# First-layer weights fetched for two column blocks at once, units in a matching order, key and value loads of two batches cut in two, and a new order for the opening

## The chip, the cores and the metric

The program runs on one core of one Trainium2 chip. The metric is the device time of one execution in microseconds (us); the time given for a kernel is the median of its runs. The engines are named as the profile names them: PE (TensorE, matrix products), DVE (VectorE), ACT (ScalarE), POOL (GpSimd) and SP (SyncE, which issues nearly all loads here).

## The reference, cut to what matters

```python
def sm_attn(qq, kk, vv):                       # softmax attention, scale = 1/8
    s = scale * np.matmul(qq, kk.transpose(0, 1, 3, 2))
    s = s - np.max(s, axis=-1, keepdims=True)
    a = np.exp(s)
    a = a / (np.sum(a, axis=-1, keepdims=True) + 1e-09)
    return np.matmul(a, vv)

p_packed = sm_attn(p, k, v)                    # q, k, v: 8 batches, 8 heads, 576, 64; p: 32 rows
out = sm_attn(q, p_packed, p_packed)
x = out.transpose(0, 2, 1, 3).reshape(4608, 512)
h = np.maximum(np.maximum(x @ w1, x @ w2), x @ w3)     # w1, w2, w3: 512 x 768
x = h @ w_out                                          # 768 x 512
...
h = x @ w_in                                           # 512 x 2048
g = np.maximum(h, 0.0) + np.log1p(np.exp(-np.abs(h)))
return g @ w_out                                       # 2048 x 512
```

All weights arrive as 64-bit floats, so each value is loaded as 8 bytes and narrowed on the chip.

## The kernel before

The attention and the first two layers run batch by batch (n = 0 to 7). For a batch, keys and queries are loaded (`load_raw`, L167), values too (`load_v`, L196). Head dimensions are brought onto the partitions: for the keys and queries of batch 0 and the keys of batch 1 (the set `BY_PE`) by PE products with the identity (L231), for all others by DVE (L253, L256). Then follow the scores of the packed rows (S, L286), the softmax (SX: DVE maximum L306, ACT exponential L312), its transposition (E, L330), the product with the values (V, L357), the scaling and transposition of the result (VS and PT, L373, L265) and the second scores (A, L286). The second softmax is a chain on DVE, ACT and POOL (AX: L397, L403, L405, L409, L423 to L434), and its result is split into a high and a low half (X, L127).

Because the packed result has only 32 rows a head, it is first multiplied into the weights of the first layer: `packed_weight_steps` (PW, L449, matmul L459) makes four 128-column blocks of "packed weights" at a time from the narrowed weights `wsb`, and splits them into `pwhi` and `pwlo`. `unit_steps` (U, L486) then makes one of 18 units, each one 128-column block f of one of the three matrices w, with 12 matmuls at L481. The maximum over the three matrices is kept in `m` (L508, L510), split into `hhi` and `hlo` (LS) and multiplied by `w_out` (L20 to L23: four column blocks of the second layer, 36 matmuls each).

The last two layers (from L959 on) follow for all batches together; the change does not touch them.

The weights come in 18 loads of 512 KB (`load_w`, L566), one for a pair (f, w): two 32-bit words a value, 256 words (1,024 bytes) in a row of the load, four rows a partition. Each is narrowed by an ACT step (L85), a POOL step (L95) and a DVE step (`combine`, L111). `w_out` comes in six loads of 512 KB (LO), with rows of 4,096 bytes. The raw loads of both share a pool of five buffers (`stp`), the raw keys and queries another of five (`rx`); so a load waits until the DVE step of the load five before it is over. All these loads stand in SP's queue.

For batch 0 and the part of batch 1 that overlaps it (called the opening here), the order of the work on every engine is written out by hand in the string `order` (L634): each word is the next step of a named piece of work (Lk10 loads keys of batch 1, heads 0; Tk10 turns them; LW21 loads a weight block, NT21 and N21 narrow it; U5 is a unit). Every engine keeps its own instructions in that order. `lead` adds idle PE products with the identity (L165) in front of a piece, `on_gpsimd` says which subtractions and products run on POOL. From batch 1 on, `small_work` (L700) sets the places of the pieces between the units.

The lines around the narrowing buffer and the units are these:

```python
wsb = wsbp.tile([P, 3 * F1, NH, P], F32, name="wsb")
c, k = divmod(3 * f + w, 4)
hi, lo = pw[n, c]
```

Of the kernel before, what the change touches and what calls it, by code (L numbers as in the profile page):

```python
# [19 lines left out]
def packed_attention_maxout_softplus(  # L20
# [22 lines left out]
    nc = tc.nc  # L43
# [107 lines left out]
    wsb = wsbp.tile([P, 3 * F1, NH, P], F32, name="wsb")  # L151
# [14 lines left out]

    def load_raw(n, g, which, queue=nc.sync):  # L167
# [5 lines left out]
        if (n, which) in BY_PE:  # L173
            queue.dma_start(
                out=t.rearrange("p t b d -> p (t b d)")[: 32 * TI, : NG * NI * D].rearrange(
                    "p (h c) -> p h c", h=NG
                ),
                in_=src[n, NG * g : NG * g + NG].rearrange("h (p r) d -> p h (r d)", r=NI),
            )
            raw[n, g, which] = t  # L180
            return
# [14 lines left out]
    def load_v(n, queue=nc.sync):  # L196
        t = vvp.tile([32 * TI, H, NI, D], F32, name="vt")
        queue.dma_start(
            out=t.rearrange("p h i d -> p h (i d)"),
            in_=v[n].rearrange("h (p r) d -> p h (r d)", r=NI),  # L200
        )
        vt[n] = t
# [246 lines left out]
    def packed_weight_steps(n, c):  # L449
# [5 lines left out]
        for g in range(NH):  # L455
            for G in range(NG):
# [3 lines left out]
                    ps[cols, G, : units * P].rearrange("p (w x) -> p w x", w=units),  # L460
                    ppT[n][rows, cols],
                    wsb[rows, 4 * c : 4 * c + units, g],
# [20 lines left out]
    def layer1_unit(n, f, w):  # L483
        every(unit_steps(n, f, w))

    def unit_steps(n, f, w):  # L486
        c, k = divmod(3 * f + w, 4)
# [78 lines left out]
    def load_w(f, w, queue=nc.sync):  # L566
        t = stp.tile([P, NH * P, 2], I32, tag="st", name="wraw")
        queue.dma_start(
            out=t.rearrange("p (g x) t -> p g (x t)", g=NH),
            in_=(w1, w2, w3)[w][:, f * 2 * P : f * 2 * P + 2 * P].rearrange(  # L570
                "(g p) x -> p g x", p=P
            ),
# [20 lines left out]
    def opening(name):  # L593
# [14 lines left out]
        if a == "U":  # L608
            return unit_steps(0, *divmod(int(num), 3))
# [22 lines left out]
    on_gpsimd.update("""AX00.sb AX00.mu AX01.mu SO5 SO0 AX10.sb AX11.sb AX10.mu X11""".split())  # L632
    lead.update({"Tk00": 11, "S0": 2, "V0": 1, "PT0": 2, "A0": 2, "Tk10": 12, "Tk13": 2, "PP1": 4, "S1": 3, "U0": 1})
    order = """  # L634
            Lk00 Lk02 Lp0 Lk01 Lk03 Lq00 Tk00 PP0 Tk00 Lq03 Tk02 PP0 Tk01 Tk02 Lq02 Lv0
# [549 lines left out]
```

## Time and profile before

| | us |
|---|---|
| median of 3 runs | 1254.85 |
| lowest and highest run | 1252.23, 1256.12 |
| the profiled execution, whole | 1258.63 |
| its span, first to last instruction | 1256.8 |
| PE busy in the span | 1240.9 (99%) |
| DVE busy in the span | 687.5 (55%) |
| PE waiting for values by DMA, its largest wait for one releaser in the first 260 us | 2.2 |

All durations below come from the profiled execution. A row of the timeline gives start, duration, engine, line, and behind it in brackets the time for which the engine stood idle and what released it. The clock column is the granted TensorE clock as a share of 2.4 GHz: 0.50 is 1.2 GHz. DMA is the mean busy share of the core's 16 DMA engines (it can pass 1 where transfers of one engine overlap).

### The profile page before, as it was taken

Reading aid. Unit: us, or ns where it says so; the run is one execution under the profiler, and the core shown is the slowest. Engines: PE = TensorE matmul, PEld = TensorE weight load, DVE = VectorE, ACT = ScalarE, POOL = GpSimd, SP = SyncE. Lnnn points to the kernel's source line nnn. Section 1 sums busy time; section 2 is a strip of 40 time slices with the busy share of each in tenths; the row PEclk is TensorE's granted clock in tenths of the full one; section 3 lists DMA queues with packets and bytes.
Section 4 is the critical chain, followed back from the end, with each engine's and each line's share of the span. In section 5 each row is a group of like instructions: output and inputs, shape, how many; then the busy total and the mean of one; then the engine's idle time right before and its main releaser. Section 6 shows DMA issues by size and latency. Waiting matters only on the chain.

```text
span 1256.8 us, 21080 instructions
## 1 busy us (share of the span) xinstructions
PE 1240.9 (99%) x8647; PEld 1065.2 (85%) x8647; DVE 687.5 (55%) x1070; ACT 463.4 (37%) x687; POOL 116.4 (9%) x112
## 2 busy tenths in 40 slices
PE   8989999999999999999999999999999999999998
PEld 6778989898999899888888888888888888888997
DVE  2965657575666649676663445634445354442443
ACT  4733443434343435454342222513224222232222
POOL 1412312122221301000000000000000000000000
PEclk9989999999999999999999999999999999999999
DMA  9967576879695722665522433415334053340641
GB/s 234 283 176 207 160 197 174 205 204 231 178 239 164 180 68 73 250 245 195 196 68 93 150 118 118 126 34 209 118 117 126 15 170 117 125 143 1 209 176 35
DMA packets 87008, 192.55 MB, mean 153 GB/s; under 512 B 12160, under 2 KB 56448, under 8 KB 81792
## 3 DMA queue, kind: packets, MB, share of 16 engines
q1 hardware_dynamic: 81920, 181.24, 48.2%
q10 hardware_dynamic: 4992, 9.96, 2.2%
q8 instruction: 68, 1.11, 0.4%
q14 instruction: 28, 0.23, 0.1%
HBM read 149.23 MB, written 41.94 MB: 152 GB/s over the span
## 4 chain that ended last, share of the span: by engine, by line
PE 94%; DMA 3%; DVE 1%; ACT 1%; issue 0%; ACTq 0%; POOL 0%; SPq 0%; DVEq 0%; POOLq 0%
PE ps L481 29%; PE ps L959 28%; PE acc L1033 10%; PE acc L1032 10%; PE acc L1031 10%; PE ps_w L459 3%; DMA qraw<-in_q_dram 2%; PE ps_s L286 1%; PE ps_v L357 1%; PE ps_e L330 1%; PE ps_k L231 1%; DMA wraw<-in_moe_w_dram 0%; DVE wsb L111 0%; DMA kraw<-in_k_dram 0%; DVE x2lo L127 0%
## 5 line engine op out<-in xcount | busy, mean ns | idle before, releaser
L959 PE MATMUL ps<-x2hi,wc 128*128 128x512 f32 (+1 forms) x1120 | 322.8, 369 | 0.0
L976 DVE TENSOR_TENSOR h<-h,ps 128x512 f32<-128x512 f32 (+1 forms) x280 | 173.9, 634 | 110.5 <-PE ps L959 105.0
L959 PEld LDWEIGHTS ps<-x2hi,wc 128*128 128x128 f32 x1120 | 203.6, 188 | 35.9
L1033 PE MATMUL acc<-w2hi,glo 128*128 128x512 f32 x576 | 224.8, 390 | 0.0
L1032 PE MATMUL acc<-w2lo,ghi 128*128 128x512 f32 x576 | 224.7, 390 | 0.0
L1031 PE MATMUL acc<-w2hi,ghi 128*128 128x512 f32 x576 | 224.1, 389 | 0.0
L959 PE MATMUL ps<-x2lo,wc 128*128 128x512 f32 (+1 forms) x560 | 206.5, 369 | 0.0
L127 DVE TENSOR_TENSOR glo<-h,ghi 128x512 fp32r<-128x512 f32 x80 | 54.9, 692 | 157.2 <-ACT ghi L125 157.2
L1032 PEld LDWEIGHTS acc<-w2lo,ghi 128*128 128x128 f32 x576 | 108.1, 188 | 23.2
L481 PE MATMUL ps<-a2hi,pwhi 128*128 128x288 f32 x576 | 127.6, 303 | 0.1
L1031 PEld LDWEIGHTS acc<-w2hi,ghi 128*128 128x128 f32 x576 | 108.2, 188 | 22.7
L1033 PEld LDWEIGHTS acc<-w2hi,glo 128*128 128x128 f32 x576 | 108.1, 188 | 22.6
L999 ACT ACTIVATE h<-h 128x1024 f32<-128x1024 f32 x40 | 42.4, 1060 | 230.2 <-DVE h L976 230.2
L481 PE MATMUL ps<-a2hi,pwlo 128*128 128x288 f32 x576 | 123.2, 296 | 0.4 <-DVE pwlo L127 0.4
L481 PE MATMUL ps<-a2lo,pwhi 128*128 128x288 f32 x576 | 123.2, 295 | 0.0
L959 PEld LDWEIGHTS ps<-x2lo,wc 128*128 128x128 f32 x560 | 105.5, 188 | 18.3
L481 PEld LDWEIGHTS ps<-a2hi,pwhi 128*128 128x128 f32 x576 | 91.6, 189 | 15.0 <-ACT m L508 5.3
L510 DVE TENSOR_TENSOR m<-ps,m 128x576 f32<-128x576 f32 x96 | 72.4, 754 | 48.9 <-PE ps L481 42.8
L481 PEld LDWEIGHTS ps<-a2hi,pwlo 128*128 128x128 f32 x576 | 92.6, 188 | 0.7 <-DVE pwlo L127 0.7
L481 PEld LDWEIGHTS ps<-a2lo,pwhi 128*128 128x128 f32 x576 | 92.5, 188 | 0.3 <-DVE a2lo L127 0.3
L127 DVE TENSOR_TENSOR pwlo<-ps_w,pwhi 128x1024 fp32r<-128x1024 f32 (+1 forms) x40 | 44.6, 1114 | 84.7 <-ACT pwhi L125 84.7
L127 DVE TENSOR_TENSOR glo<-gs,ghi 128x512 fp32r<-128x512 f32 x64 | 44.2, 691 | 79.1 <-ACT ghi L125 71.0
(105 smaller groups left out, 1495.6 us busy)
## 6 DMA issues: line engine op xcount, KB each, us to landing
wc<-wic SPq DMA_DIRECT2D x32, 1792.0 KB
qraw<-in_q_dram SPq DMA_DIRECT2D x112, 140.0 KB
wic<-wc SPq DMA_DIRECT2D x8, 1792.0 KB
kraw<-in_k_dram SPq DMA_DIRECT2D x96, 140.0 KB
vt<-in_v_dram SPq DMA_DIRECT2D x8, 1152.0 KB
wraw<-in_moe_w_dram SPq DMA_DIRECT2D x18, 512.0 KB
x2d<-xs ACTq DMA_DIRECT2D x32, 288.0 KB
xu<-x2d SPq DMA_DIRECT2D x72, 128.0 KB
```

What stands on the lines that cost most here:

```text
L127: engine.tensor_tensor(out=lo, in0=src, in1=hi.bitcast(F32), op=ALU.subtract)
L231: nc.tensor.matmul(ps[64 * G : 64 * G + 64, i // hi, c : c + rows], r[:, i, G], ident[:rows, :rows], start=True, stop=True,)
L286: nc.tensor.matmul(ps[G][cols, hh, :HS], w[rows, cols], x[rows, g, hh * HS : hh * HS + HS], start=True, stop=True,)
L459: nc.tensor.matmul(ps[cols, G, : units * P].rearrange("p (w x) -> p w x", w=units), ppT[n][rows, cols], wsb[rows, 4 * c : 4 * c + units, g ...
L481: nc.tensor.matmul(o, w, xx, start=first, stop=last)
L510: nc.vector.tensor_tensor(out=m, in0=ps[:, :, :HS], in1=ms[n, f], op=ALU.max)
L959: nc.tensor.matmul(out, l, r, start=(i == 0), stop=(i == len(terms) - 1))
L976: add(out=h[:, o], in0=h[:, a], in1=ps, op=ALU.add)
L999: nc.scalar.activation(out=out, in_=x, func=AF.Softplus)
L1031: nc.tensor.matmul(ps, ghi[:, cols], whi, start=first, stop=False)
L1032: nc.tensor.matmul(ps, ghi[:, cols], wlo, start=False, stop=False)
L1033: nc.tensor.matmul(ps, glo[:, cols], whi, start=False, stop=last)
```

## The change

- `wsb` holds two column blocks next to each other: 9 pairs d, and for each four row groups of 256 columns. `load_w(d, h)` fetches, for one matrix and a pair of column blocks, half of the 512 rows: still 18 loads of 512 KB, now with 512 words (2,048 bytes) in a row and two rows a partition.
- The units are numbered so that the two blocks of a pair alternate: unit u belongs to block `2 * (u // 6) + u % 2` and matrix `u // 2 % 3`. The splitting of a finished block (LS) moves accordingly, in all batches.
- `load_rows` cuts the loads of keys (heads pairs of batches 0 and 1) and values (batches 0 and 1) into a transfer of rows 4 p to 4 p + 3 (1,024 bytes) and one of two rows (512 bytes), where one transfer had rows of 1,536 bytes. The queries of batch 0 keep their single transfer of 1,536 bytes a row.
- `order`, `lead` and `on_gpsimd` are new. The second scores A1 now stand ahead of L20, the values product V1 ahead of the last unit, S1 behind two units, PW01 ahead of the first unit.

```diff
-    wsb = wsbp.tile([P, 3 * F1, NH, P], F32, name="wsb")
+    wsb = wsbp.tile([P, 3 * F1 // 2, NH, 2 * P], F32, name="wsb")
...
+    def load_rows(to, src, in_two, queue):
+
+        cuts = [(0, 4), (4, NI)] if in_two else [(0, NI)]
+        for a, b in cuts:
+            queue.dma_start(
+                out=to[:, :, a * D : b * D],
+                in_=src[:, 32 * TI * a : 32 * TI * b].rearrange(
+                    "h (p r) d -> p h (r d)", r=b - a
+                ),
+            )
...
+            load_rows(to, src[n, NG * g : NG * g + NG], which == "k", queue)
...
+        load_rows(t.rearrange("p h i d -> p h (i d)"), v[n], (n, "k") in BY_PE, queue)
...
-                    ps[cols, G, : units * P].rearrange("p (w x) -> p w x", w=units),
+                    ps[cols, G, : units * P].rearrange("p (w x) -> p w x", w=units // 2),
                     ppT[n][rows, cols],
-                    wsb[rows, 4 * c : 4 * c + units, g],
+                    wsb[rows, 2 * c : 2 * c + units // 2, g],
...
-    def unit_steps(n, f, w):
-        c, k = divmod(3 * f + w, 4)
+    def unit_steps(n, u):
+        f, w = 2 * (u // 6) + u % 2, u // 2 % 3
+        c, k = divmod(u, 4)
...
-    def load_w(f, w, queue=nc.sync):
+    def load_w(d, h):
         t = stp.tile([P, NH * P, 2], I32, tag="st", name="wraw")
-        queue.dma_start(
-            out=t.rearrange("p (g x) t -> p g (x t)", g=NH),
-            in_=(w1, w2, w3)[w][:, f * 2 * P : f * 2 * P + 2 * P].rearrange(
+        pair, w = divmod(d, 3)
+        nc.sync.dma_start(
+            out=t.rearrange("p (g x) t -> p g (x t)", g=2),
+            in_=(w1, w2, w3)[w][:, pair * 4 * P : pair * 4 * P + 4 * P].rearrange(
                 "(g p) x -> p g x", p=P
-            ),
+            )[:, 2 * h : 2 * h + 2],
...
-            Lk00 Lk02 Lp0 Lk01 Lk03 Lq00 Tk00 PP0 Tk00 Lq03 Tk02 PP0 Tk01 Tk02 Lq02 Lv0
+            LW10 Lk00 Lk01 Lk03 Lk02 N10 NT10 N10 Lq03 Tk00 Lp0 Tk00 Tk01 Lq00 Tk03 Tk01
...
-            if 1 <= slot <= F1:
-                layer1_split(n, slot - 1)
+            if slot == F1:
+                layer1_split(n, F1 - 1)
...
+                    if u % 6 == 5:
+                        layer1_split(n, 2 * (u // 6))
+                    elif u and u % 6 == 0:
+                        layer1_split(n, 2 * (u // 6) - 1)
```

Three places of the new order matter for what follows. The first is SP's queue at the start of the program (kraw, qraw and praw are keys, queries and packed rows of batch 0, vt the values, wraw weights). Before:

```order
L174 DMA kraw<-in_k_dram 96x2x384 x2
L207 DMA praw<-in_p_dram 128x1x64 x2
L174 DMA kraw<-in_k_dram 96x2x384 x2
L174 DMA qraw<-in_q_dram 96x2x384 x3
L198 DMA vt<-in_v_dram 96x8x384
L568 DMA wraw<-in_moe_w_dram 128x4x256
```

and now:

```order
L576 DMA wraw<-in_moe_w_dram 128x2x512
L171 DMA kraw<-in_k_dram 96x2x256
L171 DMA kraw<-in_k_dram 96x2x128
L171 DMA qraw<-in_q_dram 96x2x384
L213 DMA praw<-in_p_dram 128x1x64 x2
L171 DMA qraw<-in_q_dram 96x2x384 x3
L171 DMA vt<-in_v_dram 96x8x256
L171 DMA vt<-in_v_dram 96x8x128
L576 DMA wraw<-in_moe_w_dram 128x2x512 x6
```

One weight load has moved ahead of the keys, each of the four key loads is now the pair of rows shown once here, all four query loads stand ahead of the values, and six weight loads follow in a row.

The second place is DVE between the second scores of batch 0 (A0) and the first unit (U0): the numbered s and a are the two halves of the second softmax, wsb rows are the narrowing of weights. Before:

```order
L397 STREAM_TRANSPOSE s_442<-ps_s 128x576
L111 SCALAR_TENSOR_TENSOR wsb<-wsb,wraw 128x512
L403 TENSOR_REDUCE mx_449<-s_438 128x18
L403 TENSOR_REDUCE mx_452<-s_442 128x18
L111 SCALAR_TENSOR_TENSOR wsb<-wsb,wraw 128x512
L405 TENSOR_TENSOR s_442<-s_442,mx_452 128x576
```

and now:

```order
L403 STREAM_TRANSPOSE s_456<-ps_s 128x576
L409 TENSOR_REDUCE mx_460<-s_451 128x18
L111 SCALAR_TENSOR_TENSOR wsb<-wsb,wraw 128x512
L409 TENSOR_REDUCE mx_466<-s_456 128x18
L411 TENSOR_TENSOR s_451<-s_451,mx_460 128x576
L411 TENSOR_TENSOR s_456<-s_456,mx_466 128x576
L111 SCALAR_TENSOR_TENSOR wsb<-wsb,wraw 128x512 x2
```

Both subtractions now run on DVE, where POOL had one, and three wsb steps stand in this piece where there were two; further down both products with the reciprocal (L429 before) also move from POOL to DVE, and the count of wsb steps up to the second transposition of a (L434 before) is six instead of three.

The third place is PE at the end of the units (vt, e1T: V1; pp: PT1; wsb: PW10; ppT with vT: A1; hhi: L20). Before:

```order
L481 MATMUL ps_1075<-a2lo,pwhi 128x288 x2
L481 MATMUL ps_1075<-a2hi,pwlo 128x288 x2
L357 MATMUL ps_v<-vt,e1T 32x64 x48
L265 MATMUL ps_t<-ident,pp 128x128
L459 MATMUL ps_w<-wsb,ppT 32x512 x8
L481 MATMUL ps_1184<-hhi,wo_hi 128x288 x2
```

and now:

```order
L487 MATMUL ps_1093<-a2hi,pwlo 128x288 x2
L363 MATMUL ps_v<-vt,e1T 32x64 x48
L487 MATMUL ps_1172<-a2hi,pwhi 128x288 x2
L487 MATMUL ps_1172<-a2lo,pwhi 128x288 x2
L487 MATMUL ps_1172<-a2hi,pwlo 128x288 x2
L271 MATMUL ps_t<-ident,pp 128x128
L465 MATMUL ps_w<-wsb,ppT 32x512 x8
L292 MATMUL ps_s<-vT,ppT 32x288 x16
L487 MATMUL ps_1237<-hhi,wo_hi 128x288 x2
```

V1 has moved ahead of the last unit (its 12 matmuls are the rows of ps_1172, of which three of six are shown), and A1, which stood after the first 36 matmuls of L20, has moved ahead of them.

## Rows read from the trace of the kernel before

**Rows 1.** Busy time by stage, core 0: stretch, length, engines, PEclk, DMA share, GB/s.
```profile
0.00:24.00 24.00, 20.90 (x351) 17.08 (x352) 3.23 (x9) 9.84 (x20) 1.97 (x8) 1.00 0.93 236
24.00:40.00 16.00, 13.18 (x200) 8.72 (x200) 13.86 (x20) 10.36 (x18) 7.08 (x10) 0.90 1.07 253
76.00:85.00 9.00, 5.92 (x117) 3.54 (x117) 5.21 (x10) 2.66 (x6) 0.00 (x0) 0.63 0.63 168
85.00:89.00 4.00, 4.00 (x19) 4.00 (x19) 2.57 (x3) 0.80 (x1) 0.00 (x0) 0.54 0.02 5
160.00:480.00 320.00, 319.93 (x3301) 289.84 (x3300) 198.15 (x297) 130.26 (x206) 70.81 (x60) 1.00 0.68 180
```

**Rows 2.** What PE waited for: the opening, then everything behind it.
```profile
PE ps_v L357 <- DMA vt<-in_v_dram: 2.2, 2, 2.0
PE ps_s L286 <- ACT pT L268: 1.3, 1, 1.3
...
PE ps_s L286 <- DVE vT L256: 0.3, 1, 0.3
```

**Rows 3.** Timeline of PE at the end of the units.
```profile
75.97 0.42 PE L481 MATMUL ps<-a2hi,pwlo 128*128 128x288 f32 x2
78.44 2.79 PE L357 MATMUL ps_v<-vt,e1T 96*32 96x64 f32 x96 [2.04 <-DMA vt<-in_v_dram]
81.90 0.45 PE L265 MATMUL ps_t<-ident,pp 128*128 128x128 f32 x1 [0.68 <-DVE pp L373]
82.72 1.96 PE L459 MATMUL ps_w<-wsb,ppT 64*32 64x512 f32 x16 [0.37 <-ACT ppT L268]
84.61 0.85 PE L481 MATMUL ps<-hhi,wo_hi 128*128 128x288 f32 x2
```

**Rows 4.** The chain of work in time: the same pieces later, at full clock.
```profile
127.02 1.45 PE ps_e L330 x12
...
134.84 0.59 PE ps_w L459 x16
135.44 1.48 PE ps_v L357 x96
...
145.18 1.13 PE ps_s L286 x32
...
147.17 20.98 PE ps L481 x156
168.14 1.02 PE ps_w L459 x16
...
226.57 1.02 PE ps_w L459 x16
```

**Rows 5.** Timeline of PE in the first 41 us.
```profile
18.93 1.55 PE L357 MATMUL ps_v<-vt,e1T 96*32 96x64 f32 x96 [0.18 <-DMA vt<-in_v_dram]
...
22.22 1.18 PE L231 MATMUL ps_k<-ident,qraw 96*64 96x96 f32 x22 [0.82 <-DMA qraw<-in_q_dram]
...
24.53 2.41 PE L286 MATMUL ps_s<-vT,ppT 64*32 64x288 f32 x32
...
40.02 0.53 PE L481 MATMUL ps<-a2hi,pwhi 128*128 128x288 f32 x2
```

**Rows 6.** Groups of DVE instructions from 23 to 41 us: busy, mean ns.
```profile
L111 DVE SCALAR_TENSOR_TENSOR wsb<-wsb,wraw 128x512 int32<-128x512 int32 x5 | 4.8, 963 | 2.9 <-ACT wsb L85 2.9
...
L434 DVE STREAM_TRANSPOSE a<-s 128x576 f32<-128x576 f32 x2 | 1.5, 766 | 0.0
...
L423 DVE TENSOR_REDUCE sg<-s 128x18 f32<-128x576 f32 x2 | 1.4, 719 | 0.0
...
L127 DVE TENSOR_TENSOR pwlo<-ps_w,pwhi 128x1024 fp32r<-128x1024 f32 x1 | 1.2, 1162 | 0.0
```

**Rows 7.** Busy time by stage again: stretches with one kind of transfer.
```profile
10.00:16.00 6.00, 6.00 (x123) 4.64 (x120) 1.74 (x4) 3.02 (x7) 0.00 (x0) 1.00 1.05 234
38.00:46.00 8.00, 7.09 (x76) 6.12 (x77) 7.93 (x15) 6.65 (x15) 3.75 (x5) 1.00 0.67 208
46.00:52.00 6.00, 5.58 (x49) 4.34 (x48) 5.52 (x9) 4.53 (x7) 1.69 (x2) 1.00 1.08 358
62.00:66.00 4.00, 4.00 (x32) 4.00 (x31) 3.21 (x5) 2.61 (x5) 1.95 (x2) 1.00 1.04 381
440.00:444.00 4.00, 4.00 (x32) 4.00 (x31) 4.00 (x7) 2.08 (x3) 0.69 (x1) 1.00 0.73 192
522.00:526.00 4.00, 4.00 (x20) 3.30 (x19) 1.66 (x3) 3.03 (x5) 0.00 (x0) 1.00 0.95 339
```

**Rows 8.** Timeline of SP's queue: the issue of the values of batch 1.
```profile
64.81 0.55 SPq L198 DMA_DIRECT2D vt<-in_v_dram  x1
```

More of the change, by code (lines that the diff above doesn't have):

```diff
@@ L173, in load_raw @@
         if (n, which) in BY_PE:
-            queue.dma_start(
-                out=t.rearrange("p t b d -> p (t b d)")[: 32 * TI, : NG * NI * D].rearrange(
-                    "p (h c) -> p h c", h=NG
-                ),
-                in_=src[n, NG * g : NG * g + NG].rearrange("h (p r) d -> p h (r d)", r=NI),
+            to = t.rearrange("p t b d -> p (t b d)")[: 32 * TI, : NG * NI * D].rearrange(
+                "p (h c) -> p h c", h=NG
             )
+            load_rows(to, src[n, NG * g : NG * g + NG], which == "k", queue)
             raw[n, g, which] = t
@@ L608, in opening @@
         if a == "U":
[L609 removed]
+            return unit_steps(0, int(num))
         if a == "LS":
@@ L630, in opening @@
         }[a](*i)
[L632 to L633 removed]
+    on_gpsimd.update("""X01 LS00 LS01 SO3 LS02 SO5 LS03 LS04 SO4 AX11.sb AX10.mu AX11.mu X10 X11""".split())
+    lead.update({"Tk00": 17, "PP0": 1, "S0": 1, "PT0": 2, "A0": 1, "Tk10": 22, "Tk13": 4, "PP1": 3})
     order = """
[L635 to L653 removed]
@@ new lines, in packed_attention_maxout_softplus @@
+            N11 LW41 AX00 Tk13 AX01 LW40 N11 Tk13 AX01 NT20 LO0 PW00 N20 AX00 X01 N20
+            PW00 AX00 X01 PP1 PW01 SO2 PW00 Lq12 PP1 X00 ST2 Tk12 PW01 X00 LW51 SO2 U0
+            Tk12 NT41 PW01 LW50 SO2 N40 NT40 U1 U0 SO2 N41 N40 S1 SO0 N41 U1 ST0 LW61 U2
+            SX10 LW70 SO0 Lq13 SX10 SX11 U3 SO0 VS10 SX11 NT51 U2 LW60 E10 SO0 N51 U4 U3
+            NT50 E10 VS11 N50 N51 E11 N61 N50 LO3 U5 E11 NT61 U4 LW80 N70 NT70 LS00 PW02
+            N61 LS00 U5 LW81 U6 PW02 N70 LS01 U7 U6 PW02 LS01 LO5 Lq10 N60 NT60 U7 U8
@@ new lines, in packed_attention_maxout_softplus @@
+            SO3 ST3 N60 U9 N80 NT80 U8 LO1 SO3 PW03 Lv1 U9 N81 NT81 SO3 U10 N80 PW03 N81
+            LO4 SO3 SO5 U11 PW03 ST5 U10 PW04 Lq11 SO5 LS02 U12 Tq10 PW04 LS02 SO5 U11
+            U13 Tq12 SO5 LS03 SO1 PW04 U14 ST1 Tq13 U13 LS03 U12 U15 SO1 U14 SO1 U16 SO1
+            U15 V1 U16 Lk20 SO4 ST4 LS04 U17 SO4 LS04 VS11 SO4 VS10 PT1 Lk23 U17 PT1 SO4
+            PW10 Tq11 LS05 A1 LS05 PW10 L20 AX10 PW10 Lp2 AX10 AX11 Lk21 L20 L21 AX11
+            Lk22 AX10 AX11 AX10 AX10 AX11 AX10 AX10 AX11 L21 L22 AX11 AX11 AX10 X10 X10
@@ L654, in packed_attention_maxout_softplus @@
+            AX11 X11 X11 L22 L23 L23
     """
```

44 lines of the change are left out of this document (13 added, 31 removed).

## The prediction

> **What bounds the kernel now.** I read the stages first. From 160 to 480 us PE is busy for 319.93 of 320 us at full clock [rows 1], and over everything behind the opening PE's waits with a named releaser come to 0.3 us [rows 2]. So in the batches PE's own work is the bound, and an edit that neither adds nor removes matmuls can gain only in the opening. There the stages show the loss [rows 1]: from 0 to 24 us PE is busy 20.90 us (idle products included), from 24 to 40 us 13.18 of 16, from 76 to 85 us only 5.92 of 9 with the clock at 0.63 of 2.4 GHz, and to 89 us the clock is still 0.54. The waits say what stands behind the worst place: 2.2 us for values by DMA [rows 2]. The timeline of PE shows it [rows 3]: the last unit ends at 76.4, V1 starts at 78.44 after the values land, PT1 and PW10 each wait for one small step (0.68, 0.37 us), and at half clock V1 and PW10 take 2.79 and 1.96 us, against 1.48 and 1.02 us at full clock [rows 4].
>
> **The change, part by part.** I ask when L20 starts, and what work still lies behind it, because from there on both kernels do the same on a full PE.
>
> The front, to A0. Before, the last turning of queries starts only at 22.22, after V0 (18.93) and a wait of 0.82 us for its data, and A0 runs from 24.53 to 26.94 at half clock, 2.41 us against 1.13 [rows 4, 5]. Now all query turnings stand ahead of V0. Loads ahead of the values grow by one weight load (0.52 MB at 358 GB/s, 1.5 us [rows 7]) and one query load (0.29 MB at 234, 1.3 us) and shrink by what the cut saves on four key loads and the values (2.36 MB, 2.9 us at the prices below): V0 stays at about 19. Behind it come 1.5 us of V0, the scaling, the transposition and their two hand-overs, 1.4 us or so by the gaps in [rows 3]: A0 from 21.9 to 23.1, at full clock. That is 3.8 us earlier; with the old wait and half clock again it would be 0.
>
> From A0 to U0. This is a chain on DVE, 13.0 us before (U0 at 40.02). Now it holds six wsb steps up to the second transposition of a instead of three, and one subtraction and two products that POOL had. Three wsb steps of 0.96 us and three steps at 0.72 to 0.77 us [rows 6] are 5.1 us. Against it, one split of packed weights (1.16 us [rows 6]) moves behind the chain, and POOL's hand-overs fall away, for which I take 0.2. Net +3.7 us (bounds 2 and 5.1). So U0 stays at **40.0** (37.5 to 43): the two terms cancel.
>
> From U0 to V1. PE's work here is S1 1.13, the two transpositions E 1.45, two packed-weight products of 1.02 and one of 0.59, and 17 units of 1.61 (20.98 us for 156 matmuls, 13 units) [rows 4]: 32.6 us. PW01 (1.02) is done before U0 now; S1 came in. With 0.9 us of small waits, as before has between 40 and 76, V1 is due at 73.5, some 5 us earlier than it ran.
>
> Does the DMA keep up? The values landed at 78.4 though issued at 64.81 [rows 3, 8], so the load stream is the limit there. Its prices, per full DMA share [rows 7]: rows of 1,536 bytes (10 to 16 us, queries and values of batch 0) 234 GB/s at share 1.05, 223; rows of 1,024 (46 to 52, weights) 358 at 1.08, 331; rows of 512 (440 to 444) 192 at 0.73, 263; rows of 2,048 (522 to 526) 339 at 0.95, 357; rows of 4,096 (62 to 66, mostly) 381 at 1.04, 366. Keys and values of two batches are 4.72 MB: 21.2 us in one piece; cut, 3.15 MB at 331 and 1.57 MB at 263 are 15.5 us. That saves 5.7 us (0 to 6.9). The weights, 9.44 MB, go from 331 to 357: 2.1 us (0 to 2.7). Two query loads move ahead of the values, 1.15 MB at 223, +5.1; one load of w_out moves behind, 0.52 MB at 366, -1.4. In the stretch from 38 to 46 us the share is 0.67, 2.6 us empty because loads waited for buffers that DVE frees; with more wsb steps done by then I take back half, 1.3. Values land at 78.4 - 5.7 - 2.1 + 3.7 - 1.3 = **73.0** (70 to 82). V1 is due at 73.5: in time by a hair, so I charge 0.5 us.
>
> [...]
>
> From V1 to L20. V1 1.48, the last unit 1.61 (it covers the scaling), PT1 0.33, a hand-over 0.4, PW10 1.02, A1 1.13: L20 starts at 73.5 + 0.5 + 6.0 = 80.0. Before, it started at 84.61 with A1 (1.13) still ahead and about 4 us at half clock to come (clock 0.54 to 89 us [rows 1]), worth 1.9: the same point is 87.6. Gain **7.6 us**. What is late next: the last queries of batch 1 land after the values and must be turned before A1; the chain from A1 to the next batch's first unit, some 14 us, lies beside 19 us of second layer.
>
> Edits at nothing. The alternating units, later splits and two-block `wsb` cost PE nothing: the same 12 matmuls a unit, the same columns. A block's maximum and split end one unit later; the second layer needs blocks 4 and 5 only after four others, 24 of 36 matmuls or 3.2 us, which covers a DVE, an ACT and a POOL step. If that cover were gone, each batch would lose up to a microsecond, 7 in all; DVE is busy 198 of 320 us there [rows 1], so I keep zero.
>
> **Own time and median.** The profiled execution took 1258.63 us: its sum is 1251.0. The median run is 3.8 us shorter. Only the opening has waits that can differ between runs, so the profiled run may hold more of them than most; I take 1.1 us off the gain. Forecast 1254.85 - 6.5 = **1248.4 us**.
>
> **Rivals.**
> 1. Cut rows are no cheaper. Then values land at 78.7, V1 waits 5 us, and, as before after a wait of 2 us, the clock falls (78.4 to 88.7 us before, about 4 us of loss, some inside the wait). Gain 7.6 - 4.7 - 2.5, near 0: 1254. For it: total DMA busy share is near 1 throughout, and I have no row with 1,024 and 512 bytes mixed. Against: three stretches with other row sizes give 263 to 357.
> 2. The front is longer: a wsb step on DVE stands ahead of the softmax steps and waits for its weight load, or the half clock falls between 24 and 40 us. Price 2.5 to 4 us: 1251.5. For it: wsb steps waited 2.9 us for ACT there [rows 6]. Against: 3.8 us of A0's gain is a floor under it.
> 3. Slower: smaller transfers starve the DMA. In SP's program each load waits for the one eight places before it. Up to the values of batch 1 there were 46 loads of 407 KB on average, now 63 of 307 KB, so at most 2.5 MB are in flight instead of 3.3. The values needed 13.6 us from issue to use [rows 3, 8]; if a transfer takes 10.5 us from issue to landing, the stream falls to 240 GB/s and the 19.8 MB up to the values end at about 84.5. V1 is then 11 us late, with half clock 14: 1254.85 + 7 = 1262. It decides from about 255 GB/s down. Against: the stages up to 40 us hold 236 and 253 GB/s with waits in them [rows 1], and a stretch of weights alone reaches 358.
> 4. The change does nothing visible, because the last weights rather than the values hold PE up one place earlier: PW04 is due at about 63.5. That is rival 1's time.
>
> **How the numbers follow.** Forecast 0.55 (1245 to 1251), rivals 1 and 4 together 0.2 (1252 to 1257), rival 2 0.13 (1250 to 1253), rival 3 0.12 (1257 to 1264). A difference under 0.3%, 3.8 us, cannot be told from none here: faster means below 1251.1, slower above 1258.6. Faster: nearly all of the first and under half of rival 2, 0.6. Same: 0.28. Slower: 0.12. The lower end, 1243.5, has the DMA bounds at their best and U0 at 37.5, less the charge; the upper, 1256, leaves out rival 3.
>
> **What would show it.** Right: V1 at 72 to 75 us with little wait, L20 near 80, no stretch of half clock around it, U0 near 40, key and value stretches near 300 GB/s, batches unchanged at 58.4 us each (168.14 to 226.57 [rows 4]). Wrong: U0 after 42; PE waits at L465 or L363 for wraw or vt; the granted clock at 0.5 anywhere from 24 to 90 us; waits at L487 in later batches.

## The result, and the profile of the changed kernel

The changed kernel takes 1261.21 us (median of 7 runs, 1257.3 to 1262.45), the kernel before 1254.05 beside it (7 runs, 1251.92 to 1257.5): ratio 1.0052, 95% interval 1.0034 to 1.007. It is slower by 6.5 us by this ratio (7.2 by the medians), where 6.5 us less were forecast. Its profiled execution took 1259.91 us, with a span of 1257.9.

The stages of after, core 0 (columns as in [rows 1]; the last row is another stretch, in which the cut values of batch 1 and the queries move):

```profile
0.00:24.00 24.00, 19.43 (x348) 17.28 (x348) 2.75 (x7) 10.27 (x22) 1.43 (x8) 1.00 0.94 235
24.00:40.00 16.00, 12.59 (x146) 8.90 (x154) 13.85 (x24) 7.54 (x13) 5.77 (x8) 0.73 1.07 285
76.00:85.00 9.00, 6.69 (x126) 6.18 (x125) 3.38 (x5) 2.10 (x4) 2.46 (x2) 0.86 0.98 192
85.00:89.00 4.00, 3.47 (x56) 2.11 (x54) 3.68 (x6) 2.99 (x6) 2.83 (x3) 0.88 0.70 200
160.00:480.00 320.00, 320.00 (x3294) 288.98 (x3294) 189.84 (x297) 130.52 (x206) 65.58 (x59) 1.00 0.67 180
72.00:78.00 6.00, 6.00 (x46) 5.92 (x45) 4.05 (x6) 3.94 (x7) 5.28 (x4) 1.00 1.15 190
```

From 160 to 480 us PE is full as before, so the loss lies in the opening. From 24 to 40 us PE does less than in [rows 1] (12.59 us, clock 0.73 against 0.90), although the DMA moves more (285 GB/s against 253).

PE in after, from the first scores to the second, and the first unit:

```profile
13.49 1.21 PE L292 MATMUL ps_s<-vT,pT 64*32 64x288 f32 x32 [0.44 <-ACT pT L274]
...
21.41 1.09 PE L363 MATMUL ps_v<-vt,e1T 96*32 96x64 f32 x60 [0.40 <-DMA vt<-in_v_dram]
24.28 0.31 PE L363 MATMUL ps_v<-vt,e1T 96*32 96x64 f32 x4 [1.79 <-issue]
...
26.01 2.11 PE L292 MATMUL ps_s<-vT,ppT 64*32 64x288 f32 x32 [0.15 <-ACT ppT L274]
...
32.47 1.21 PE L237 MATMUL ps_k<-ident,kraw 96*64 96x96 f32 x24 [1.80 <-DMA kraw<-in_k_dram]
...
39.54 1.96 PE L465 MATMUL ps_w<-wsb,ppT 64*32 64x512 f32 x16
...
44.23 0.53 PE L487 MATMUL ps<-a2hi,pwhi 128*128 128x288 f32 x2
```

V0 is over at 24.6 us (20.5 in [rows 5]), A0 runs at half clock (0.54) from 26.0 to 28.1, and the first unit starts at 44.23 instead of 40.02. At the end of the units:

```profile
78.93 0.65 PE L363 MATMUL ps_v<-vt,e1T 96*32 96x64 f32 x32
81.89 1.40 PE L363 MATMUL ps_v<-vt,e1T 96*32 96x64 f32 x64 [2.31 <-DMA vt<-in_v_dram]
83.22 0.85 PE L487 MATMUL ps<-a2hi,pwhi 128*128 128x288 f32 x2
83.86 0.68 PE L487 MATMUL ps<-a2lo,pwhi 128*128 128x288 f32 x2
...
86.45 0.30 PE L271 MATMUL ps_t<-ident,pp 128*128 128x128 f32 x1 [0.16 <-DVE pp L379]
87.12 1.09 PE L465 MATMUL ps_w<-wsb,ppT 64*32 64x512 f32 x16 [0.37 <-ACT ppT L274]
88.00 1.18 PE L292 MATMUL ps_s<-vT,ppT 64*32 64x288 f32 x32
89.11 0.53 PE L487 MATMUL ps<-hhi,wo_hi 128*128 128x288 f32 x2
```

V1 starts at 78.93, then waits 2.31 us for the second transfer of its values, and the last unit behind it runs at half clock (0.68 us a row against 0.43). In before, at a clock of 0.50, twelve products of 288 columns took 2.89 us (85.25 to 88.14), 1.2 columns a ns; that is what the traces show of the 1.2 GHz of the clock column. L20 starts at 89.1; the same point was 87.6 in the profiled execution of before, and 80.0 was forecast for after.

What lies behind that point is nearly the same in all executions. The table takes the start of L20 with A1 done (1.13 us added where A1 comes later, and 1.9 for the half clock of [rows 1]):

| execution | span | the point | behind it |
|---|---|---|---|
| before, as on record | 1256.8 | 87.6 | 1169.2 |
| after | 1257.9 | 89.1 | 1168.8 |
| before with half of the values (below) | 1251.3 | 81.9 | 1169.4 |
| after with two query loads moved back (below) | 1253.4 | 83.7 | 1169.7 |

In nine other traces that reach L20 at full clock the last column lies between 1167.8 and 1169.9. So a time can be turned into this point, to about 1 us: a median of 1254.3 (119 timed runs of before) is a span of about 1252.5 and the point at 83.2; 1261.2 is 90.

### The profile page after: what moved, and what is told of

Same layout as the page of the kernel before. It is cut to its first block, busy times and chain, and to the rows that moved or that the text cites. A ratio compares the mean times of both kernels' runs of the same rounds, so it can differ in the third digit from the quotient of the medians.

```text
span 1257.9 us, 21084 instructions
## 1 busy us (share of the span) xinstructions
PE 1240.4 (99%) x8659; PEld 1065.9 (85%) x8659; DVE 671.7 (53%) x1065; ACT 463.5 (37%) x687; POOL 122.4 (10%) x117
## 4 chain that ended last, share of the span: by engine, by line
PE 94%; DMA 4%; ACT 1%; issue 0%; DVE 0%; SPq 0%; ACTq 0%; POOL 0%; DVEq 0%; POOLq 0%
PE ps L487 29%; PE ps L972 28%; PE acc L1046 10%; PE acc L1045 10%; PE acc L1044 10%; PE ps_w L465 3%; DMA woraw<-in_moe_w_out_dram 2%; PE ps_s L292 1%; DMA kraw<-in_k_dram 1%; PE ps_v L363 1%; DMA wraw<-in_moe_w_dram 1%; PE ps_e L336 1%; PE ps_k L237 1%; DMA vt<-in_v_dram 1%; PE ps_t L271 0%
## 5 line engine op out<-in xcount | busy, mean ns | idle before, releaser
L127 POOL TENSOR_TENSOR hlo<-m,hhi 128x576 fp32r<-128x576 f32 x46 | 69.9, 1520 | 284.9 <-ACT hhi L125 284.3
```

The lines of the kernel that those rows point to most:

```text
L127: engine.tensor_tensor(out=lo, in0=src, in1=hi.bitcast(F32), op=ALU.subtract)
```

## Experiments: the cut and the loads alone

Every ratio below is to runs of before taken beside the run; their medians differ from set to set (1253.4 to 1255.3 us), so small differences are safer read from the ratios.

After without the cut (nocut), and before with the cut alone:

```
-        cuts = [(0, 4), (4, NI)] if in_two else [(0, NI)]
+        cuts = [(0, NI)]
```

> The changed kernel with one transfer of 1,536-byte rows a key or value load, as before; all else as changed. If the cut rows are cheaper, as the prediction had it (309 against 223 GB/s), undoing the cut makes the load stream 5.7 us longer: values of batch 1 land near 87 us instead of 81.5 and the time rises by 4 to 6 us, to about 1266. If the cut rows cost as much a byte or more (the stretch with the cut values of batch 1, 72 to 78 us, moved 186 to 193 GB/s in the changed kernel) and only add transfers, the values land 0 to 3 us earlier and the time falls by 1 to 4 us, to about 1258. If the loss lies in the order alone, nothing changes: within 1 us of 1261.

Measured: 1260.87 us (10 runs), ratio to before 1.0047 (1.0032 to 1.0062), against 1.0052 with the cut. In its profile V1 starts 1.5 us before the 81.89 of after, not 5.7 us behind it:

```profile
80.42 1.55 PE L363 MATMUL ps_v<-vt,e1T 96*32 96x64 f32 x96 [2.06 <-DMA vt<-in_v_dram]
```

> The kernel before with nothing changed but the cut of the key and value loads of batches 0 and 1 into 1,024 and 512 bytes a row. Cheaper rows: values land up to 5.7 us earlier, the wait of 2.0 us at V1 and the half clock behind it go, 1248 to 1250. Rows at the same price: V1 starts where it did or up to 3 us later, 1254 to 1258.

Measured: 1255.27 us (12 runs), ratio 1.0009 (0.9994 to 1.0025). In neither kernel does the cut cost or give anything clear of noise: of the 5.7 us that the prediction gave it, none is seen. The test is nocut: in before, earlier values give no time back either (below), so the second run alone could not have shown cheaper rows.

The loads alone, in stretches of one kind, up to eight in flight; nothing of the reference is computed:

> Loads alone, twelve stretches one after the other with up to eight transfers in flight; attention and layers are left out and the output is zeros. Prices by stretch in GB/s. If row length decides: 1,536-byte rows near 223, 1,024 near 331, 512 near 263, 2,048 near 357 whatever they load. If the number of partitions decides (keys and values go to 96 partitions, weights to 128): 96-partition loads near 200 to 230 at 1,536 and at 1,024 bytes a row, 128-partition loads of the same values near 330 at both.

Stretches of that run (DVE, POOL, clock, DMA share, GB/s). In order: values of 96 partitions in rows of 1,536 bytes, of 1,024, of 512; values of 128 partitions in rows of 1,536 and of 1,024; weights, always 128 partitions, in rows of 1,024 and of 2,048; keys of 96 partitions in one piece and cut; queries as batch 1 loads them, 32 partitions and rows of 4,480 bytes:

```profile
4.00:20.00 16.00, 0.45 (x3) 0.00 (x0) 1.00 1.10 220
49.00:60.00 11.00, 0.45 (x3) 0.00 (x0) 1.00 1.12 245
65.00:77.00 12.00, 0.90 (x6) 0.00 (x0) 1.00 1.21 223
81.00:92.00 11.00, 0.46 (x3) 0.00 (x0) 1.00 1.06 392
96.00:108.00 12.00, 0.46 (x3) 0.00 (x0) 1.00 1.09 371
112.00:128.00 16.00, 1.54 (x10) 0.00 (x0) 1.00 1.09 350
133.00:148.00 15.00, 1.54 (x10) 0.00 (x0) 1.00 1.05 389
153.00:168.00 15.00, 1.95 (x13) 0.00 (x0) 1.00 1.08 255
174.00:190.00 16.00, 3.90 (x26) 0.00 (x0) 1.00 1.09 258
204.00:216.00 12.00, 2.17 (x16) 0.00 (x0) 1.00 0.90 189
```

The number of partitions sets the price: 220 against 392 GB/s for the same rows of 1,536 bytes. Row length moves it by a tenth or so. (Spread over 128 partitions, the values of one partition also lie next to each other in memory; the rows of the weights do not, and reach 350 and 389.) In [rows 7] the two went together: the keys, queries and values of batch 0 use 96 partitions, weights 128.

## Experiments: weights and units

After with each weight load of one column block again (1,024 bytes a row):

```
-            out=t.rearrange("p (g x) t -> p g (x t)", g=2),
+            out=t.rearrange("p (g x) t -> p g (x t)", g=NH),
```

> The kernel after with one part undone: each weight load again takes one column block of all 512 rows (1,024 bytes a row) into the narrowing buffer of before; the order, the units and the cut loads stay. Theory row length (the prediction: rows of 1,024 bytes cost 8% more): the weights need 2 us more, 1262 to 1263. Theory partitions (the loads alone on the chip showed 350 GB/s for 1,024 and 389 for 2,048 bytes at 128 partitions each): 1261 to 1263. Theory weights (the load of two half blocks is what costs the 6 us, since the kernel before with only this and the units' order changed ran at 1261): back to 1255 to 1257. Theory order (the opening's new order and the alternating units cost it): 1261.

Measured: 1261.61 us (6 runs), ratio 1.0059 (1.0044 to 1.0074). The form of the weight loads moves nothing that the time shows.

The same, with the units also numbered as before, in the opening and in the batches:

```
-        f, w = 2 * (u // 6) + u % 2, u // 2 % 3
+        f, w = divmod(u, 3)
```

> The kernel after with one-block weight loads (which alone moved nothing) and with the units numbered as before, the three matrices of one column block in a row, in the opening and in the batches; the opening's order, the cut loads, idle products and POOL steps stay those of the kernel after, only the splits of blocks 0 and 2 move forward to where these blocks are now finished. Theory units (two blocks under way at once hold up DVE, the buffers of the running maximum and the last splits): back to 1254 to 1257. Theory order (the new order of the opening, first unit at 44 and V1 near 80 us, is the cost whatever the units are): 1260 to 1262.

Measured: 1260.6 us (8 runs), ratio 1.0046 (1.003 to 1.0062). In the kernel after the alternating units cost nothing clear of noise.

The kernel before with two-block weights and alternating units in its own order (the diff shows the end, where the splits LS04 and LS05 now come together):

```
- U17 SO1 SO3 U15 SO1 SO2 Lq12 V1 U16 SO2 U17 SO2 Lq13 VS11 LS05 VS10
+ U17 SO1 SO3 U15 SO1 SO2 Lq12 V1 U16 LS04 SO2 U17 LS05 LS04 SO2 Lq13 LS05 VS11 VS10
```

> The kernel before with its own order, idle products and POOL steps, and only the weights and units changed: weight loads of two column blocks (2,048 bytes a row) and the units numbered in alternating blocks, the splits moved to where the blocks are finished; keys and values in one piece. Theory front or order: it stays at 1254, within 1 us. Theory weights (a block needs two loads before its first unit, its maximum and split end later, and the opening or the batches pay): 1257 to 1262, with waits of PE at the units or the packed-weight products, or waits at the units in later batches. Were rows of 2,048 bytes 8% cheaper, as the prediction had it, V1 would wait less and the time be 1252 to 1253.

Measured: 1261.23 us (6 runs), ratio 1.0055 (1.0039 to 1.0071). That looked like the whole loss of the change. Its profile names another cause, two rows of PE and then three of DVE:

```profile
77.90 1.55 PE L363 MATMUL ps_v<-vt,e1T 96*32 96x64 f32 x96
82.42 0.45 PE L271 MATMUL ps_t<-ident,pp 128*128 128x128 f32 x1 [2.98 <-DVE pp L379]
...
79.64 0.75 DVE L517 TENSOR_TENSOR m<-ps,m 128x576 f32<-128x576 f32 x1
80.30 1.58 DVE L127 TENSOR_TENSOR hlo<-m,hhi 128x576 fp32r<-128x576 f32 x2
81.81 0.47 DVE L379 TENSOR_SCALAR pp<-ps_v,rc 128x64 f32<-128x64 f32 x2
```

PT1 waits 3.0 us for the scaling, which stands on DVE behind two hlo steps, and then runs at half clock. The order had been written so for this run; it is not the order of the kernel after. With the scaling first:

```
- U16 LS04 SO2 U17 LS05 LS04 SO2 Lq13 LS05 VS11 VS10
+ U16 SO2 U17 SO2 Lq13 VS11 VS10 LS04 LS05
```

> The kernel before with two-block weight loads and alternating units, as in the run at 1261.2 us, but with the scaling behind V1 now ahead of the splits of the last two blocks on DVE. In that run's profile PT1 waited 3.0 us for the scaled result, behind two hlo steps on DVE. Theory last splits (alternating units finish two blocks at the very end, and their splits stand ahead of the scaling): PT1's wait falls under 1 us and the time to 1256 to 1258. Theory units otherwise (running maxima, weights later): 1260 to 1262.

Measured: 1256.93 us (12 runs), ratio 1.0025 (1.0012 to 1.0039): 4.3 us from the place of the two splits. The 2.7 us that remain were not followed up; its profile shows waits for wsb (2.1 us, before the last packed weights) and still 1.5 us for the scaling.

## Experiments: the values of batch 1

Before, unchanged, profiled once more:

> The kernel before, unchanged, profiled a second time. Its profiled run on record is 1258.63 us, while the median of 39 runs is 1254.9 and their lowest 1251.9; its mean granted clock is 0.994, and over the runs the clock lies between 0.994 and 0.999, higher where the run is shorter. Theory of a run-to-run stall: a run near 1254 shows V1 without the half clock from 78.4 to 88.7 us, the values landing before V1, and L20's comparable point some 4 us earlier than 87.6, near 83; then most of what the prediction took for removable is not there in the typical run. Rival: the typical run has the same stall at V1, and is shorter elsewhere (the last layers, or the time around the span).

Measured: 1262.02 us, once more not a typical execution. V1 waits 3.2 us and the clock is at half for 10 us behind it. The 119 timed runs of before have a median of 1254.27 and a median granted clock of 0.998, which is 2 x 0.002 x 1252 = 5 us of half clock in all; the profiled execution on record has 0.994, 15 us. So the stall at V1 was suspected to be one of some executions only. Half of the values (heads 4 to 7 use those of batch 0) in both kernels:

```
+        if n == 1:
+            t = vt[1] = vt[0]
+            ... the load over heads 0 to 3 alone
```

> The kernel before, with only half of the values of batch 1 loaded (heads 0 to 3; heads 4 to 7 use those of batch 0): 0.59 MB less, so the rest lands some 2 to 2.5 us earlier. Theory stall in the profile only (the timed runs of before have a mean granted clock near 0.998, about 5 us of half clock in all, and so no half clock of 10 us behind V1): the median stays within 1 us of 1254. Theory of the prediction (V1's wait of 2 us and the half clock of 10 us behind it are there in every run): 1249 to 1250.

Measured: 1253.36 us (12 runs), ratio 0.9991 (0.9978 to 1.0003).

> The kernel after, with only half of the values of batch 1 loaded (both transfers over heads 0 to 3; heads 4 to 7 use those of batch 0): 0.59 MB less, landing some 2 to 2.5 us earlier. Theory values (V1's wait of 2.3 us by DMA is a cost of the kernel after in the timed runs too): 1257.5 to 1259. Theory order (the units end late and the next small waits, pp and the queries behind the values, take the place): 1260 to 1261.

Measured: 1256.84 us (12 runs), ratio 1.0012 (0.9996 to 1.0028).

In before the earlier values change nothing clear of noise, in after they give 4.4 us back by the medians, 5.0 by the ratios (1.0052 to 1.0012). The profile of the first shows what an undisturbed end of the units looks like:

```profile
76.81 1.55 PE L364 MATMUL ps_v<-vt,e1T 96*32 96x64 f32 x96
79.05 0.30 PE L272 MATMUL ps_t<-ident,pp 128*128 128x128 f32 x1 [0.69 <-DVE pp L380]
79.72 1.09 PE L466 MATMUL ps_w<-wsb,ppT 64*32 64x512 f32 x16 [0.37 <-ACT ppT L275]
80.75 0.53 PE L488 MATMUL ps<-hhi,wo_hi 128*128 128x288 f32 x2
```

Against [rows 3], V1 starts 1.6 us earlier, stays at full clock, and L20 comes at 80.75 instead of 84.61.

Why are the values late in after? First try, the values ahead of a query load and a load of w_out in SP's queue:

```
- LO5 Lq10 N60 ... SO3 PW03 Lv1 U9
+ LO5 Lv1 Lq10 N60 ... SO3 PW03 U9
```

> The kernel after, with both transfers of the values of batch 1 moved ahead of the query load of heads 0 and 1 (and so ahead of one load of w_out). Theory values: they land some 2.5 us sooner, V1 starts on time near 79 without the wait of 2.3 us and without the half clock from 82.5 to 86.0, L20 starts near 86.5 instead of 89.1, and the time falls by 2 to 3 us, to about 1258.5. Theory front (the units simply start 4 us late and all later work follows): V1's wait goes as well but returns as another wait (the query turning or the queries behind the values, before A1), time 1260 to 1261. Nobody expects less than 1256 from this edit alone.

Measured: 1265.09 us (5 runs), ratio 1.0081 (1.0068 to 1.0094). A miss for both theories: V1 no longer waits, but the queries behind the values come later, and DVE turns them early. One row of DVE:

```profile
78.63 0.78 DVE L259 STREAM_TRANSPOSE vT<-qraw 128x576 f32<-128x576 f32 x1 [7.36 <-DMA qraw<-in_q_dram]
```

The running maxima stand behind that turning, and a unit of PE waited 6.6 us for one of them. Second try: two query loads behind the values, as in before, their turning behind the first step of PW10, and A1, which needs them, back in the second layer:

```
- PW00 Lq12 PP1 ... SO0 Lq13 SX10 ... PW03 Lv1 U9 ... PW04 Lq11 ... U13 Tq12 ... Tq13 ... A1 ... L20
+ PW00 PP1 ... SO0 SX10 ... PW03 Lv1 Lq12 U9 ... PW04 Lq13 Lq11 ... Tq12 ... L20 Tq13 ... A1
```

> The kernel after with two query loads of batch 1 (heads 2 and 3) moved back behind the values of batch 1, as in the kernel before, their turning back behind PW10, and A1 back into the first block of the second layer. Theory values (after's V1 waits because 1.15 MB of queries went ahead of the values, priced at 5.1 us in the prediction): the values land by 77 us, V1 runs on time near 79 without its wait of 2.3 us and without the half clock behind it, and the time falls by about 4 us, as with half of the values: 1257. Theory total (the same bytes must land before A1 in any order): A1 waits for queries instead, 1260 to 1261.

Measured: 1257.73 us (12 runs), ratio 1.0013 (0.9998 to 1.0027): 3.5 us back by the medians, 4.9 by the ratios, as with half of the values. The PE rows of its profiled execution, which took 1255.51 us and so is one of its shorter ones:

```profile
76.60 1.55 PE L363 MATMUL ps_v<-vt,e1T 96*32 96x64 f32 x96
...
80.83 0.30 PE L271 MATMUL ps_t<-ident,pp 128*128 128x128 f32 x1 [0.90 <-DVE pp L379]
81.49 1.09 PE L465 MATMUL ps_w<-wsb,ppT 64*32 64x512 f32 x16 [0.37 <-ACT ppT L274]
82.52 0.54 PE L487 MATMUL ps<-hhi,wo_hi 128*128 128x288 f32 x2
```

V1's second part had started at 81.89; now all of V1 runs at 76.60 in one piece, and no half clock stands near it. With half of the values giving the same, V1's late values are about half of the loss by the medians and three quarters by the ratios, and the queries ahead of them make them late. The run moved the turnings and A1 too, so the loads are not shown alone.

## Experiments: the front, and two tries for a better kernel

What is left, 1.5 to 3.5 us, should sit before the first unit. Four edits of the front, by their diffs: the first weight load behind the values of batch 0; more idle products ahead of the key turnings; one subtraction and two products of the softmax on POOL as before, on top of half of the values; the last two together, on top of the moved query loads:

```
- LW10 Lk00 Lk01 Lk03 Lk02 N10 NT10 N10
+ Lk00 Lk01 Lk03 Lk02 ... LW71 LW10 ... N30 N10 NT10 N10
...
- "Tk10": 22, "Tk13": 4
+ "Tk10": 36, "Tk13": 12
...
- on_gpsimd X01 LS00 ...
+ on_gpsimd AX00.sb AX00.mu AX01.mu X01 LS00 ...
```

> The kernel after, with its first weight load (and the narrowing of it) moved from the head of SP's queue to behind the values of batch 0. In the profiled runs S0 starts at 13.49 us instead of 11.84, V0 ends at 24.6 instead of 20.5 and the first unit starts near 44.2 instead of 40.0. Theory front (the loads ahead of keys and values set the whole opening): S0 near 12, V0 done near 23, first unit near 42.7, and the time falls by 1.5 us, to about 1259.7. Theory values (V1 waits for the values of batch 1, whatever runs ahead of it): the front moves the same, but V1's wait grows from 2.3 to nearly 4 us and the time stays at 1261. Theory order (the new order as such, through DVE, POOL and the idle products, is the cost): S0 moves, the first unit doesn't, 1261.

Measured: 1263.22 us (6 runs), ratio 1.0065 (1.005 to 1.0079). S0 came at 11.84 and V0 at 18.70, but the first unit at 46.4: PE waited 3.65 us for the keys of batch 1, and DVE 0.69 and 1.47 us for the narrowing of weights. Two rows of PE show also that V0, begun 1.65 us sooner, ended only 0.7 us sooner:

```profile
20.49 1.09 PE L363 MATMUL ps_v<-vt,e1T 96*32 96x64 f32 x60 [1.14 <-DMA vt<-in_v_dram]
23.60 0.31 PE L363 MATMUL ps_v<-vt,e1T 96*32 96x64 f32 x4 [2.02 <-issue]
```

> The kernel after, with 36 idle products ahead of the first turning of batch 1's keys instead of 22, and 12 ahead of the turning of heads 3 instead of 4, so that PE does not stand idle for 1.8 and 0.9 us there. Theory clock (the half clock from 34.75 to 41.58 us in the kernel after costs the first unit 1.5 to 2 us, by PW00 at 1.96 us and key turnings at half speed): no half clock there, first unit near 42.5, time 1259.5. Theory front (the keys land when they land, and DVE's chain ends at 44 anyway): the clock holds, the first unit stays within 0.7 us of 44.2, time 1261. Theory values: first unit earlier, V1's wait longer, time 1261.

Measured: 1261.04 us (6 runs), ratio 1.0044 (1.0028 to 1.006). The clock held from 30 us on and the first unit came at 42.9, but units then waited 1.5 and 1.2 us for packed weights and V1 1.15 us for values: what the front gained was waited later.

> The kernel after with half of the values of batch 1 (1256.84 us, where V1 no longer waits), and with one subtraction and both products of the second softmax of batch 0 on POOL, as in the kernel before. This tells what the DVE chain before the first unit costs once the values are out of the way. In after's profile the chain from the first transposition (28.2) to the last a2lo (45.1) takes 16.9 us, in before's 13.0. Theory chain: 2 us earlier units, 1255. Theory keys (PW00 ends at 41.5 because its PE place is behind late keys, so the first unit does not move): 1256.5 to 1257. The hand-overs to POOL could also make it slower: 1258.

Measured: 1257.08 us (12 runs) against 1256.84 without the POOL steps: nothing.

> The kernel after with two query loads behind the values (1257.7 us), and on top of it the two edits meant for its front, together: 36 and 12 idle products ahead of the key turnings, so that the clock does not fall there, and one subtraction and two products of the softmax on POOL as before. The first unit stood at 43.2 us in that run's profile, at 40.0 in the kernel before. Theory front (what is left of the difference, 2 to 3 us, is the later first unit): first unit near 41.5, 1256. Theory loads (the keys and weights that PW00 and DVE wait for land when they land, since the DMA is full there): first unit stays at 42.5 to 43.5, 1257 to 1258.

Measured: 1258.83 us (12 runs), ratio 1.0035 (1.0021 to 1.0049) against 1257.73 and 1.0013 without the two edits: no gain. In its profiled execution (1262.93 us, the longest of the twelve) the first unit came at 46.4, after a wait of 2.6 us for packed rows by DMA. What sets the first unit in the kernel after is thus not settled. That the full DMA (share 1.07 from 24 to 40 us) brings keys and weights late fits the waits, but it was only argued.

Two tries to take the good part into the kernel before. First seven idle products before the last query turning, the values ahead of a load of w_out, and V1 ahead of the last unit; then V1 ahead of the last unit alone:

```
- LO3 Lv1 SO4 ... LS04 U17 SO1 SO3 U15 ... Lq12 V1 U16 SO2 U17 SO2 Lq13 VS11 LS05 VS10
+ Lv1 LO3 SO4 ... LS04 V1 SO1 SO3 U15 ... Lq12 U17 VS11 VS10 U16 SO2 PT1 U17 SO2 Lq13 LS05
```

> The kernel before with three small edits taken from what the runs showed: seven idle products ahead of the last turning of queries (PE waits 0.7 us there, and A0 behind it ran at half clock, 2.4 us against 1.2), V1 ahead of the last unit as in the kernel after (so that the unit covers the scaling, 0.7 us, and the transposition's copy, 0.4 us), and the values of batch 1 one load earlier. Theory typical run (V1's values land in time, as the run with half of the values showed: no change of time there): 1.1 us from V1 and up to 1.2 us from A0, so 1252. Theory values (they land between 75 and 77, so an earlier V1 waits and the clock falls): 1254 to 1257.

Measured: 1260.29 us (7 runs), ratio 1.0044 (1.0026 to 1.0061). Another miss of the same kind: PE took V1 at 75.05, but the scaling stood on DVE behind the narrowing of w_out, whose load had been put back. DVE, then PE:

```profile
78.21 1.29 DVE L111 SCALAR_TENSOR_TENSOR wo<-wo,woraw 128x512 int32<-128x512 int32 x2 [5.68 <-POOL woraw L95]
...
81.91 0.45 PE L265 MATMUL ps_t<-ident,pp 128*128 128x128 f32 x1 [3.52 <-DVE pp L373]
```

> The kernel before with V1 ahead of the last unit, as in the kernel after, and the scaling right behind it on DVE; nothing else is moved. The earlier try of this also put the values ahead of a load of w_out, and DVE then waited 5.7 us for that load with the scaling behind it. Theory cover (the last unit hides the scaling and the copy, 1.1 us, and the values land by 75): 1253. Theory values (they land only just in time for V1 near 76.8, so V1 waits where the last unit stood): 1254 to 1255. If the wait lowers the clock: 1256 to 1258.

Measured: 1255.92 us (12 runs), ratio 1.0007 (0.9993 to 1.0021): nothing. No version was found that beats the kernel before.

## Why the prediction was wrong, point by point

**The price by row length: the step that failed first.** "Keys and values of two batches ... cut ... saves 5.7 us" came from full-share prices that [rows 7] seemed to give by row length. The stretches compared differed in partitions too, and the runs show that this is what counts: 220 to 258 GB/s for 96 partitions whatever the rows, 350 to 392 for 128. So 223 against 331 did not speak for a cut: at 96 partitions rows of 512, 1,024 and 1,536 bytes moved 223, 245 and 220 GB/s. Uncut, the values were in use 1.5 us sooner and the time was the same. The size of a load does not show: at 128 partitions loads of 512 KB reach 389 GB/s and loads of 1,152 KB 392. Without the cut's term the prediction's own sum, 78.4 - 2.1 + 3.7 - 1.3, is 78.7 and, without the credits for the weights and the stalls, 82.1; V1's second part started at 81.89. That is an agreement of sums: no run took the credit for the stalls by itself, and for the weights the loads alone bear the cheaper rows out (350 and 389 GB/s), but with one-block weights V1's second part came at 81.40, not 2.1 us behind 81.89. The term of the moved queries, +5.1, was of the right size: with them moved back all of V1 starts at 76.60 without a wait, so its values were there at least 5.3 us sooner. Its price was taken from rows of 1,536 bytes, another kind of load; alone these loads moved 189 GB/s, which for 1.15 MB is 6.1 us.

**The starting point.** "Own time and median" took 1.1 us off the gain. The median says that the common point of a timed run is at 83.2, not 87.6, and half of the values, which takes the stall away, gains nothing clear of noise in timed runs. Of the 7.6 us of gain, 4.4 (87.6 less 83.2) were a matter of the execution that had been profiled. Even with every other step right the gain would have been about 3 us, and the time 1251. The difference of 3.8 us between profile and median stood in the text; taken off whole, it would have been near the 4.4.

**A0 earlier by 3.8 us.** It ran from 26.0 to 28.1 at half clock instead of 21.9 to 23.1. The keys came 1.6 us later behind the weight load (S0 at 13.49; at 11.84 in the run that puts this load back), the values of batch 0 by 2.5 us: with the cut no cheaper, the loads ahead of V0 had only grown, and the 2.9 us taken off for it there were missing. Then PE stood for 1.79 us before the last four products of V0, a stop that the sum did not have (last section).

**The DVE chain: +3.7 us.** From the first transposition of the scores to the first unit it was 13.0 us (27.01 to 40.02 [rows 5]) and is 16.0 (28.23 to 44.23): 3.0 more, the mechanism and nearly the size. The first two rows are the starts in before and after; the others, of DVE in after, answer to [rows 6]:

```profile
27.01 1.45 DVE L397 STREAM_TRANSPOSE s<-ps_s 128x576 f32<-128x576 f32 x2 [0.63 <-PE ps_s L286]
28.23 1.45 DVE L403 STREAM_TRANSPOSE s<-ps_s 128x576 f32<-128x576 f32 x2 [0.48 <-PE ps_s L292]
...
L111 DVE SCALAR_TENSOR_TENSOR wsb<-wsb,wraw 128x512 int32<-128x512 int32 x6 | 4.0, 681 | 1.0 <-POOL wraw L95 1.0
L411 DVE TENSOR_TENSOR s<-s,mx 128x576 f32<-128x576 f32 x2 | 1.9, 982 | 0.0
L435 DVE TENSOR_TENSOR s<-s,rc 128x576 f32<-128x576 f32 x2 | 1.6, 791 | 0.0
```

A wsb step cost 0.68 us instead of 0.96, and waits of about 1 us came in. So "the two terms cancel" failed by A0 alone, whose end came 1.2 us later than before instead of 3.8 us earlier, and U0 came at 44.2. This is rival 2, at 4 us.

**From U0 to V1.** 34.7 us against 33.5: right within small waits (0.7 us for packed weights).

**Edits at nothing.** Right for the kernel after, within noise: PE is full from 160 to 480 us, and the old numbering of units gave nothing back that is clear of it. In another order the same edit cost several microseconds, through the place of two splits.

**The rivals.** Rival 1, no cheaper rows, came true together with rival 2. The prediction priced each alone, at 1254 and 1251.5; with both V1 is due later and waits all the same, and the gain counted against them was too large. By its own prices, a gain of 3.2 us (the point from 83.2 to 80.0) less 7.2 for rival 1 and up to 4 for rival 2 is a time of 1258 to 1262. Rival 3 gave nearly the measured time, but not by its mechanism: up to V1 the DMA moved 257 GB/s in after and 259 in before, not the 240 that it needs, and larger transfers (no cut) were no faster (1260.87 us against 1261.21). That each load waits for the one eight places before it shows in the trace of before: the load eight behind the values of batch 1 was issued at 78.32, after 5.2 us of waiting for them. Rival 4 did not appear: no packed-weight product waits between U0 and V1 in after.

The account of the 6.5 us (7.2 by the medians): 3.5 to 5 are V1's late values and the half clock behind them, shown by two runs; the remaining 1.5 to 3.5 lie before V1, where the first unit is 4 us late and V1 ahead of the last unit gives some back. That last part is read from the traces, not shown by a run.

## What to carry to other kernels

Before a price per byte is put down to one property of a transfer, look for a second property that changes with it; a kernel of loads alone, one kind after the other, tells them apart. A profiled execution longer than the median must be explained before its stalls are spent as gain, and the mean granted clock of the timed runs is a cheap test of it. On a full DMA a load moved ahead of another was paid by that other to the full here (one weight load: keys 1.6 us later; two query loads: values at least 5.3 us later), and a small step on an engine that keeps its order cost what stood behind it (two splits ahead of the scaling: 4.3 us).

## What the hardware showed that was not expected

**Partitions.** 96 partitions reach 220 to 258 GB/s and 128 reach 350 to 392, at about the same busy share of the DMA engines (1.08 to 1.21 and 1.05 to 1.09), so the share does not show the loss. 32 partitions reach 189 at 0.90. Why the partitions count so, no run here shows.

**PE's 349th product.** In 18 of 19 traces of the opening PE stands still before the same product in the order of its program, number 349 or 350, for 0.24 to 2.7 us, and no engine or load that the profile names releases it. In before that product is in the last turning of queries, and in after it is in V0:

```profile
23.63 0.35 PE L231 MATMUL ps_k<-ident,qraw 96*64 96x96 f32 x2 [0.24 <-issue]
```

It starts between 23.3 and 26.4 us in all 18, also where V0 had begun at 18.7 us. In two traces product 222 shows the same, 127 products earlier; with its weight load each product is two instructions, 254 in all.

The traces point to what PE waits for there. Besides the loads, their DMA record has a queue of instructions, in before and after alike:

```profile
q8 instruction: 68, 1.11, 0.4%
```

These are 68 packets of 16,384 bytes, and PE runs 8,647 products and as many weight loads in before, 254 of these instructions for each packet, as many as lie between products 222 and 349: by this count the queue brings PE's program. In all 18 traces PE goes on 2.4 to 2.9 us after the second of these packets has begun (21.0 and 23.63 us in before, 21.7 and 24.28 in after). In the 19th trace that packet begins earliest, at 20.25 us, product 349 starts 2.4 us later as well, and PE need not stop. Where PE stops before product 222, the first packet had begun 2.9 and 3.0 us before; in the other 17 traces it lies 4.6 us or more before that product, and PE does not stop. By these times PE waits for its own program, a reading of the traces that no run tested, and the delay stands in the front of both kernels: 0.24 us in the trace of before, 1.79 in that of after. Why the second packet begins when it does, and what the wait costs in timed runs, was not tried.
